# W1 in halves of five DMAs, epsilon folded into the statistics, the last tile in three pieces, 1/den spread by DMA: four edits to a fused attention and MLP kernel

## Chip, cores, metric

The kernel runs on one core of one Trainium2 chip. The metric is the device time of one execution in microseconds (us), lower is better. Each execution also has a span, from the first to the last instruction of the core; for nearly every kernel here the time is about 1.7 us more than the span of the same run.

## The reference

```python
# x: [1, 2048, 640] bf16; wqkv [640, 1920]; wo [640, 640]; w1 [640, 1536]; w2 [1536, 640]; 32 heads of 20
xn = layernorm(x, eps=1e-5)                      # no scale, no bias
q, k, v = split_heads(xn @ wqkv)
phi = lambda t: where(t > 0, t + 1, exp(t)) + 1e-6
kv  = einsum("bhsd,bhse->bhde", phi(k), v)
z   = phi(k).sum(over s)
att = (phi(q) @ kv) / (phi(q) . z + 1e-6)        # "den" is the denominator
out = x + att @ wo + (gelu(xn @ w1 + b1) @ w2 + b2)
```

## The kernel before

Tokens are cut into 16 tiles of 128 rows, and into 4 chunks of 4 tiles. A small recording layer puts each instruction on one of five engines in program order and adds semaphore waits where a resource that it reads or writes has another engine as its last user. A later instruction of an engine never overtakes an earlier one.

Loads. W1 comes in four quarters of its 1536 columns (480 KB each, rows of 768 B), the first on ScalarE's queue, the others between the x tiles on SyncE's:

```python
NW1 = 4
FW = F // NW1
def dma_w1(i, eng="sync"):
    dma_w(eng, W1[:, :, i * FW:(i + 1) * FW], w1v[:, :, i * FW:(i + 1) * FW], r_W1[i])
dma_x(0, 1)
dma_w("scalar", b1tmp[:], ..., r_b1tmp)
dma_w1(0, "scalar")
dma_x(1, 1)
dma_w1(1)
dma_x(2, 1)
dma_w1(2)
dma_x(3, 1)
dma_w1(3)
dma_x(4, 2)
...
```

Layernorm of a tile: two `bn_stats` and a `bn_aggr` on VectorE, then epsilon and the power -1/2 on POOL, then the normalize on VectorE. `ln_next(t)` puts the statistics of tile t+1 ahead of the normalize of tile t:

```python
def ln_aggr(t):
    s = t % 4
    Pl.ins(v, lambda e: e.bn_aggr(aggr[:, s, :], stats[:, s, :]), ...)
    Pl.ins(g, lambda e: e.tensor_single_scalar(veps[:, s:s + 1], aggr[:, s, 1:2], EPS, ALU.add), ...)
    Pl.ins(g, lambda e: e.tensor_tensor(out=rstd[:, s:s + 1], in0=veps[:, s:s + 1],
                                        in1=mhalf[:], op=ALU.pow), ...)
def ln_next(t):
    if t + 1 < NT:
        ln_half(t + 1, 0); ln_half(t + 1, 1)     # bn_stats, waits for x tile t+1
    ln_norm(t)
    if t + 1 < NT:
        ln_aggr(t + 1)
```

The first stage on TensorE (PE): ten warm-up matmuls, then transposes of normalized tiles and "units". A unit is five matmuls that make 128 columns of the hidden layer, followed by a Gelu on ScalarE. A unit waits for the portion of W1 that holds its columns. The first three units are `h_first`; tile 2 is transposed only after units 6 and 7:

```python
filler(10)
ln_stats(0); ln_half(1, 0); ln_half(1, 1); ln_aggr(1)
norm0(...)            # normalize of tile 0 in two parts, after tile 1's statistics
... transposes of tile 0 ...
b1_step()
ln_norm(1)
h_first([0, 1, 2])
xnT_copy(1, transp(1))
ln_stats(2); ln_next(2)                  # statistics(2), statistics(3), normalize(2)
units(0, 1, 3, 2 * JQ)                   # JQ = 3: tile 0, units 3 to 5
units(1, 1, 0, 2 * JQ)                   # tile 1, units 0 to 5
units(0, 2, 2 * JQ, 2 * JQ + 2)          # tiles 0 and 1, units 6 and 7
xnT_copy(2, transp(2))                   # the transposes of tile 2
units(0, 2, 2 * JQ + 2, JT)
```

The last stage adds, per token tile, 12 W2 matmul pairs and 5 attention matmul pairs into two PSUM banks. Before a chunk's attention matmuls its phi(q), held in `PQ`, is multiplied by 1/den, which a matmul with the 0/1 matrix `E4` spreads from 32 partitions to 128:

```python
def rden_step(c, b):
    Pl.ins("tensor", lambda e: e.matmul(bank(b), E4[:, c, :], rden[:], start=True, stop=True), ...)
    Pl.ins("scalar", lambda e: e.activation(rs, bank(b), ACT.Copy), ...)
    for j in range(DT):
        Pl.ins(v, lambda e, j=j: e.tensor_tensor(out=PQ[:, j, cc], in0=PQ[:, j, cc], in1=rs, op=ALU.mult), ...)
def out_last(t):                          # the last tile, in two halves of 320 columns
    for h in range(2):
        ... 17 matmuls, one addition with x, one output DMA ...
for (waits, fns, ev, dma) in list(Pl.records["sync"]):
    if dma and ev is not None:
        Pl.wait_event("sync", ev)         # at the end SyncE waits for every DMA it issued
```

Of the kernel before, what the change touches and what calls it, by code (L numbers as in the profile page):

```python
# [112 lines left out]
def bass_parallel_sum__linear_attn_block__dense_activation_gelu__prompt_kernel(  # L113
# [23 lines left out]
    with contextlib.ExitStack() as es:  # L137
# [34 lines left out]
        veps = sb("veps", [P, 4], FP32)  # L172
# [34 lines left out]
        NW1 = 4  # L207
        r_W1 = [R_("W1_%d" % i) for i in range(NW1)]
# [3 lines left out]
        r_stats = [R_("stats%d" % i) for i in range(4)]  # L212
        r_aggr = [R_("aggr%d" % i) for i in range(4)]
        r_veps = [R_("veps%d" % i) for i in range(4)]
# [26 lines left out]
        def dma_w1(i, eng="sync"):  # L241
            dma_w(eng, W1[:, :, i * FW:(i + 1) * FW], w1v[:, :, i * FW:(i + 1) * FW], r_W1[i])
        dma_x(0, 1)
        dma_w("scalar", b1tmp[:], B_b1.rearrange("(a p) -> a p", p=P), r_b1tmp)
        dma_w1(0, "scalar")
        dma_x(1, 1)
        dma_w1(1)
        dma_x(2, 1)
        dma_w1(2)
        dma_x(3, 1)  # L250
        dma_w1(3)
# [59 lines left out]
        def ln_half(t, h):  # L311
            s = t % 4
            Pl.ins(v, lambda e: e.bn_stats(stats[:, s, 6 * h:6 * h + 6], x_in[:, t, h * HW:(h + 1) * HW]),  # L313
                   reads=[r_x[t]], writes=[r_stats[s]])

        def ln_aggr(t):
            s = t % 4
            Pl.ins(v, lambda e: e.bn_aggr(aggr[:, s, :], stats[:, s, :]),
                   reads=[r_stats[s]], writes=[r_aggr[s]])
            Pl.ins(g, lambda e: e.tensor_single_scalar(veps[:, s:s + 1], aggr[:, s, 1:2], EPS, ALU.add),  # L320
                   reads=[r_aggr[s]], writes=[r_veps[s]])
            Pl.ins(g, lambda e: e.tensor_tensor(out=rstd[:, s:s + 1], in0=veps[:, s:s + 1],
                                                in1=mhalf[:], op=ALU.pow),
                   reads=[r_veps[s], r_small], writes=[r_rstd[s]])
# [27 lines left out]
        def h_unit(t0, n, jb):  # L352
# [6 lines left out]
                reads=[r_W1[jb * P // FW]] + r_xnT[t0:t0 + n], writes=[B_[b]])  # L359
# [22 lines left out]
        def h_first(jbs):  # L382
            bs = [take(1) for _ in jbs]
            for (ks, res) in (((0, 1), r_xnTA), ((2, 3, 4), r_xnT[0])):
                for jb, b in zip(jbs, bs):
                    Pl.ins("tensor", [(lambda e, k=k, jb=jb, b=b: e.matmul(
                        bank(b, 0, P), W1[:, k, jb * P:(jb + 1) * P], xnT[:, k, 0:P],
                        start=(k == 0), stop=(k == DT - 1))) for k in ks],
                        reads=[r_W1[jb * P // FW], res], writes=[B_[b]])
# [20 lines left out]
        b1_step()  # L410
# [23 lines left out]
        units(0, 1, 3, 2 * JQ)  # L434
        units(1, 1, 0, 2 * JQ)
        units(0, 2, 2 * JQ, 2 * JQ + 2)
        xnT_copy(2, transp(2))
        units(0, 2, 2 * JQ + 2, JT)
        ln_next(3)
        ln_next(4)  # L440
        units(2, 1, 0, JQ)
        xnT_copy(3, transp(3))
        units(2, 1, JQ, JT)
# [40 lines left out]
        Pl.ins(v, lambda e: e.memset(KVT, 0.0), writes=[r_KVT] + r_W1)  # L484
        for f in range(DT):
            b = take(2)
            for t in range(NT):
# [5 lines left out]
                   reads=B_[b:b + 2], writes=[r_GT[f]] + r_W1)  # L493
# [71 lines left out]

        def rden_step(c, b):
            cc = slice(c * CW, (c + 1) * CW)
            s = c % 3
            rs = ek[:, s, 0:CW]
            Pl.ins("tensor", lambda e: e.matmul(bank(b), E4[:, c, :], rden[:], start=True, stop=True),  # L570
                   reads=[r_E4, r_rden], writes=[B_[b]])
            Pl.ins("scalar", lambda e: e.activation(rs, bank(b), ACT.Copy), reads=[B_[b]], writes=[r_ek[s]])  # L572
            for j in range(DT):
                Pl.ins(v, lambda e, j=j: e.tensor_tensor(out=PQ[:, j, cc], in0=PQ[:, j, cc], in1=rs, op=ALU.mult),  # L574
                       reads=[r_ek[s], r_PQ[c][j]], writes=[r_PQ[c][j]])

        def x_again(c):
            src = xv[c * CW:(c + 1) * CW, :].rearrange("(t p) d -> p t d", p=P)
            Pl.ins("sync", lambda e: e.dma_start(x_res[:, c * CH:(c + 1) * CH, :], src),
                   writes=[r_xr[c]] + r_xnT, dma=True)  # L580
# [15 lines left out]

        def mm(b, t, i, h):
            tok = slice(t * P, (t + 1) * P)
            l, r = ((HG[:, i, tok], W2[:, i, :]) if i < JT else (PQ[:, i - JT, tok], Msb[:, i - JT, :]))
# [25 lines left out]
        def out_last(t):  # L625
            b = take(2)
            xb(t)
            for h in range(2):
                hs = slice(h * HW, (h + 1) * HW)
                Pl.ins("tensor", [mm(b, t, i, h) for i in range(JT + DT)],  # L630
                       reads=[r for i in range(JT + DT) for r in mm_reads(t, i)], writes=[B_[b + h]])
                Pl.ins(v, lambda e, h=h, hs=hs: e.tensor_tensor(
                    out=out_sb[:, h, 0:HW], in0=bank(b + h, 0, HW), in1=x_res[:, t, hs], op=ALU.add),
                    reads=[B_[b + h], r_xb[t]], writes=[r_out[h]])
                Pl.ins("sync", lambda e, h=h, hs=hs: e.dma_start(ov[t * P:(t + 1) * P, hs], out_sb[:, h, 0:HW]),
                       reads=[r_out[h]], dma=True)
# [5 lines left out]
        out_w2(2, JT // 2, JT, bs[2])  # L642
        for t in range(3):
            out_fin(t, bs[t])
        for t in range(3, NT - 1):
            b = out_w2(t)
            if t in (3, 6, 10):
                rden_step({3: 1, 6: 2, 10: 3}[t], take(1))
            out_fin(t, b)
        out_last(NT - 1)  # L650

        for (waits, fns, ev, dma) in list(Pl.records["sync"]):
            if dma and ev is not None:
                Pl.wait_event("sync", ev)
# [36 lines left out]
```

## Time and profile before

| kernel before | us |
|---|---|
| time, median of the first three runs | 211.89 (211.79 to 212.27) |
| the profiled run: time, span | 212.41, 210.7 |
| PE busy | 205.5 (98%) |
| transposes of tile 2 start | 12.32 |
| last PE instruction ends | 207.80 |

The page of the kernel before, its first and fourth parts: busy time of each engine, and the chain of work that ended last, as shares of the span.

```profile
PE 205.5 (98%) x1585; PEld 140.1 (67%) x1585; DVE 110.5 (52%) x226; ACT 76.8 (36%) x145; POOL 20.5 (10%) x61
PE 86%; DVE 7%; DMA 4%; SPq 1%; issue 1%; DVEq 0%
```

PE is the bound, so a microsecond counts only where PE waits, where PE has fewer instructions, or after PE's end. PE waits at the start. The timeline of the kernel before, first 14 us (start, length, engine, line, operation, out<-in, shapes, count; in brackets the idle time before it and what ended that):

```profile
4.51 0.23 POOL L320 TENSOR_SCALAR veps<-aggr 128x1 f32<-128x1 f32 x1 [2.80 <-DVE aggr L318]
4.82 0.57 POOL L322 TENSOR_TENSOR rstd<-veps,mhalf 128x1 f32<-128x1 f32 x1
5.34 0.21 DVE L318 BATCH_NORM_AGGREGATE aggr<-stats 128x2 f32<-128x12 f32 x1
5.47 0.71 DVE L369 TENSOR_SCALAR xn_tm<-xPK,aggr,rstd 128x256 bf16<-128x256 bf16 x2
5.83 0.29 PE L376 MATMUL ps<-ident,xn_tm 128*128 128x128 bf16 x2
...
6.63 1.22 PE L386 MATMUL ps<-xnT,W 128*128 128x128 bf16 x15
7.68 0.44 PE L340 MATMUL ps<-ident,xn_tm 128*128 128x128 bf16 x5
8.48 3.78 PE L356 MATMUL ps<-xnT,W 128*128 128x128 bf16 x55 [0.35 <-DMA W<-in_B_w_dram]
...
10.88 1.02 DVE L313 BATCH_NORM_STATS2 stats<-xPK 128x6 f32<-128x320 bf16 x2 [0.69 <-DMA xPK<-in_A_x_dram]
11.82 0.43 DVE L333 TENSOR_SCALAR xn_tm<-xPK,aggr,rstd 128x640 bf16<-128x640 bf16 x1
...
12.32 0.45 PE L340 MATMUL ps<-ident,xn_tm 128*128 128x128 bf16 x5
```

Read it backwards from 12.32: the transposes of tile 2 wait for its normalize (11.82), which stands in VectorE's order behind the statistics of tile 3 (10.88), which waited for x tile 3 to land. PE itself was just done with its units. At 8.48 PE had waited 0.35 us for W1's second quarter. The normalize of tile 0 (5.47) starts as soon as tile 1's aggregation (5.34) lets it; its rsqrt (4.82 + 0.57 = 5.39) was only just ready as well.

The end of the chain of waits of the kernel before (start, length, what):

```profile
141.20 0.21 PE ps L570
141.41 8.96 PE ps L600 x66
150.38 0.22 PE ps L570
...
164.45 0.22 PE ps L570
...
183.14 0.22 PE ps L570
183.35 24.46 PE ps L600 x180
...
207.84 0.49 DVE out_sb L632
```

L570 is the spreading matmul. It is on the chain four times, between gapless matmuls. After the last addition the output DMA was issued by 208.69 and landed at 209.94; then SyncE was still going through its waits until 210.23, and the span ended at 210.66.

### The profile page before, as it was taken

Reading aid. Unit: us, or ns where it says so; the run is one execution under the profiler, and the core shown is the slowest. Engines: PE = TensorE matmul, PEld = TensorE weight load, DVE = VectorE, ACT = ScalarE, POOL = GpSimd, SP = SyncE. Lnnn points to the kernel's source line nnn. Section 1 sums busy time; section 2 is a strip of 40 time slices with the busy share of each in tenths; the row PEclk is TensorE's granted clock in tenths of the full one; section 3 lists DMA queues with packets and bytes.
Section 4 is the critical chain, followed back from the end, with each engine's and each line's share of the span. In section 5 each row is a group of like instructions: output and inputs, shape, how many; then the busy total and the mean of one; then the engine's idle time right before and its main releaser. Section 6 shows DMA issues by size and latency. Waiting matters only on the chain.

```text
span 210.7 us, 3883 instructions
## 1 busy us (share of the span) xinstructions
PE 205.5 (98%) x1585; PEld 140.1 (67%) x1585; DVE 110.5 (52%) x226; ACT 76.8 (36%) x145; POOL 20.5 (10%) x61
## 2 busy tenths in 40 slices
PE   7999999999999999999999999999999999999994
PEld 2689987444457777777666555677777777777772
DVE  4689981000008888999078866468451522263221
ACT  2579887666676554111253575110100100100000
POOL 2244557700000000000000000000000000000000
PEclk9999999999999999999999999999999999999999
DMA  5994758999000000000000000355411010001011
GB/s 165 340 349 99 101 111 101 347 321 346 10 0 0 0 3 0 0 3 0 0 0 3 0 5 0 124 138 170 163 35 54 9 65 31 31 31 34 31 62 33
DMA packets 21787, 17.46 MB, mean 83 GB/s; under 512 B 8713, under 2 KB 21769, under 8 KB 21769
## 3 DMA queue, kind: packets, MB, share of 16 engines
q1 hardware_dynamic: 21088, 16.72, 27.6%
q10 hardware_dynamic: 680, 0.49, 0.9%
q8 instruction: 12, 0.20, 0.4%
q14 instruction: 7, 0.05, 0.1%
HBM read 12.62 MB, written 2.62 MB: 72 GB/s over the span
## 4 chain that ended last, share of the span: by engine, by line
PE 86%; DVE 7%; DMA 4%; SPq 1%; issue 1%; DVEq 0%
PE ps L600 35%; PE ps L356 23%; PE ps L477 10%; PE ps L488 10%; PE ps L510 5%; DMA xPK<-in_A_x_dram 4%; DVE PQ L467 3%; DVE ek L465 1%; DVE W L534 1%; SPq L232 1%; PE ps L530 1%; PE ps L546 1%; DVE ZB L524 1%; PE ps L556 1%; DVE stats L313 0%
## 5 line engine op out<-in xcount | busy, mean ns | idle before, releaser
L600 PE MATMUL ps<-W,HG 128*128 128x320 bf16 x384 | 54.9, 299 | 0.0
L356 PE MATMUL ps<-xnT,W 128*128 128x128 bf16 (+2 forms) x435 | 52.0, 282 | 0.4 <-DMA W<-in_B_w_dram 0.4
L600 PEld LDWEIGHTS ps<-W,HG 128*128 128x128 bf16 x384 | 37.5, 98 | 15.2 <-issue 0.4
L356 PEld LDWEIGHTS ps<-xnT,W 128*128 128x128 bf16 x435 | 35.5, 98 | 16.1 <-DMA W<-in_B_w_dram 0.5
L360 ACT ACTIVATE HG<-ps,b1c 128x128 bf16<-128x128 f32 (+2 forms) x87 | 40.0, 492 | 13.2 <-PE ps L356 11.1
L465 DVE TENSOR_SCALAR ek<-ek 128x512 bf16<-128x512 bf16 (+1 forms) x36 | 10.9, 304 | 40.2 <-ACT ek L464 39.1
L464 ACT ACTIVATE ek<-ps 128x512 bf16<-128x512 f32 (+1 forms) x36 | 23.2, 644 | 20.4 <-PE ps L510 11.2
L619 DVE TENSOR_TENSOR out_sb<-ps,xnT 128x640 bf16<-128x640 f32 x15 | 12.4, 825 | 29.3 <-PE ps L600 26.2
L600 PE MATMUL ps<-Msb,PQ 128*128 128x320 bf16 x160 | 24.2, 299 | 0.0
L510 PE MATMUL ps<-xnT,Wqkv 128*128 128x512 bf16 x100 | 22.1, 379 | 0.0
L477 PE MATMUL ps<-Wqkv,xnT 128*128 128x320 bf16 x160 | 21.9, 299 | 0.0
L488 PE MATMUL ps<-xPK,xn_tm 128*128 128x320 bf16 x160 | 21.9, 299 | 0.0
L572 ACT ACTIVATE ek<-ps 128x512 bf16<-128x512 f32 x4 | 2.4, 597 | 49.2 <-PE ps L570 49.2
L600 PEld LDWEIGHTS ps<-Msb,PQ 128*128 128x128 bf16 x160 | 15.6, 98 | 6.3
L477 PEld LDWEIGHTS ps<-Wqkv,xnT 128*128 128x128 bf16 x160 | 15.7, 98 | 6.2
L488 PEld LDWEIGHTS ps<-xPK,xn_tm 128*128 128x128 bf16 x160 | 15.7, 98 | 6.1
L510 PEld LDWEIGHTS ps<-xnT,Wqkv 128*128 128x128 bf16 x100 | 11.6, 118 | 9.5 <-issue 0.2
L313 DVE BATCH_NORM_STATS2 stats<-xPK 128x6 f32<-128x320 bf16 x32 | 15.2, 475 | 3.5 <-DMA xPK<-in_A_x_dram 2.9
L467 DVE SCALAR_TENSOR_TENSOR PQ<-ps,ek 128x512 bf16<-128x512 f32 x20 | 13.8, 692 | 2.1
L467 DVE SCALAR_TENSOR_TENSOR xPK<-ps,ek 128x640 bf16<-128x640 f32 x16 | 13.2, 825 | 1.7
L498 DVE TENSOR_TENSOR Msb<-Msb,xPK 128x640 f32<-128x640 f32 x14 | 11.6, 825 | 0.5
L574 DVE TENSOR_TENSOR PQ<-PQ,ek 128x512 bf16<-128x512 bf16 x20 | 7.1, 419 | 9.0 <-ACT ek L572 9.0
(64 smaller groups left out, 89.3 us busy)
## 6 DMA issues: line engine op xcount, KB each, us to landing
xnT<-in_A_x_dram SPq DMA_DIRECT2D x4, 640.0 KB, 4.1
Wqkv<-in_A_wqkv_dram SPq DMA_DIRECT2D x3, 800.0 KB, 6.9
out_dram<-out_sb SPq DMA_DIRECT2D x15, 160.0 KB, 1.8
W<-in_B_w_dram SPq DMA_DIRECT2D x1, 1920.0 KB, 15.3
W<-in_B_w_dram SPq DMA_DIRECT2D x3, 480.0 KB, 7.6
xPK<-in_A_x_dram SPq DMA_DIRECT2D x2, 640.0 KB, 9.3
Wo<-in_A_wo_dram SPq DMA_DIRECT2D x1, 800.0 KB, 10.5
xPK<-in_A_x_dram SPq DMA_DIRECT2D x4, 160.0 KB, 4.5
```

Source lines behind the costliest of these rows:

```text
L313: Pl.ins(v, lambda e: e.bn_stats(stats[:, s, 6 * h:6 * h + 6], x_in[:, t, h * HW:(h + 1) * HW]), reads=[r_x[t]], writes=[r_stats[s]])
L356: Pl.ins("tensor", [(lambda e, k=k: e.matmul(bank(b, 0, w), W1[:, k, jb * P:(jb + 1) * P], xnT[:, k, tok], start=(k == 0), stop=(k == DT - ...
L360: Pl.ins("scalar", lambda e: e.activation(HG[:, jb, tok], bank(b, 0, w), ACT.Gelu_apprx_tanh, bias=b1c[:, jb:jb + 1]), reads=[B_[b], r_b1c ...
L464: Pl.ins("scalar", lambda e: e.activation(e2, src, ACT.Exp), reads=br, writes=[r_ek[s]])
L465: Pl.ins(v, lambda e: e.tensor_scalar(et, et, 1.0, 1e-6, ALU.min, ALU.add), reads=[r_ek[s]], writes=[r_ek[s]])
L467: Pl.ins(v, lambda e: e.scalar_tensor_tensor(out=d2, in0=src, scalar=0.0, in1=e2, op0=ALU.max, op1=ALU.add), reads=br + [r_ek[s]], writes= ...
L477: fns.append(lambda e, k=k, h=h, b=b, t=t: e.matmul(bank(b + h, 0, HW), xnT[:, k, t * P:(t + 1) * P], Wqkv[:, k, D + h * HW:D + (h + 1) * ...
L488: Pl.ins("tensor", [(lambda e, t=t, h=h, b=b, f=f: e.matmul(bank(b + h, 0, HW), xn_tm[:, t, f * P:(f + 1) * P], PK[:, t, h * HW:(h + 1) * ...
L498: Pl.ins(v, lambda e, t=t: e.tensor_tensor(out=zsum, in0=zsum, in1=PK[:, t, :], op=ALU.add), reads=[r_PK[t], r_zsum], writes=[r_zsum])
L510: Pl.ins("tensor", [(lambda e, k=k, j=j, b=b: e.matmul(bank(b), Wqkv[:, k, j:D:DT], xnT[:, k, cc], start=(k == 0), stop=(k == DT - 1))) fo ...
L600: return lambda e: e.matmul(bank(b + h, 0, HW), l, r[:, h * HW:(h + 1) * HW], start=(i == 0), stop=(i == JT + DT - 1))
L619: Pl.ins(v, lambda e: e.tensor_tensor(out=halves(out_sb[:, s, :]), in0=pair(b), in1=halves(x_res[:, t, :]), op=ALU.add), reads=B_[b:b + 2] ...
```

## The change

Its intent: fewer, longer rows for W1 and single 128-row slices for the first units to wait on; one POOL step less between aggregation and rsqrt; three PE matmuls less; a shorter end. The diff, cut to its core:

```diff
-        NW1 = 4
-        r_W1 = [R_("W1_%d" % i) for i in range(NW1)]
+        NW1 = 2
+        r_W1 = [[R_("W1_%d_%d" % (i, k)) for k in range(DT)] for i in range(NW1)]
...
-        def dma_w1(i, eng="sync"):
-            dma_w(eng, W1[:, :, i * FW:(i + 1) * FW], w1v[:, :, i * FW:(i + 1) * FW], r_W1[i])
+        def dma_w1(i):
+            for k in range(DT):
+                dma_w("sync", W1[:, k, i * FW:(i + 1) * FW], w1v[:, k, i * FW:(i + 1) * FW], r_W1[i][k])
         dma_x(0, 1)
-        dma_w1(0, "scalar")
         dma_x(1, 1)
+        dma_w1(0)
+        dma_x(2, 1)
         dma_w1(1)
-        dma_x(2, 1)
-        dma_w1(2)
         dma_x(3, 1)
-        dma_w1(3)
...
         def ln_half(t, h):            # after bn_stats of the first half
+            if h == 0:
+                Pl.ins(g, lambda e: e.tensor_single_scalar(stats[:, s, 2:3], stats[:, s, 2:3], D * EPS, ALU.add), ...)
         def ln_aggr(t):
-            Pl.ins(g, ... veps = aggr + EPS ...)
             Pl.ins(g, ... rstd = pow(...)) # now of aggr itself
...
         # h_first: waits for the slices W1[i][k] that it reads; b1_step moved behind its matmuls
-        units(0, 2, 2 * JQ, 2 * JQ + 2)    # JQ = 3
+        units(0, 2, JQ, JQ + 2)            # JQ = 6: the same units
...
+        def rden_dma(c):
+            for i in range(4):
+                Pl.ins("sync", lambda e, i=i: e.dma_start(rdb(c)[i:P:4, :], rden[H * c:H * (c + 1), :]), ...)
         def x_again(c):
-                   writes=[r_xr[c]] + r_xnT, dma=True)
+                   writes=[r_xr[c]] + (r_xnT if c == 0 else []), dma=True)
...
         def out_last(t):
-            for h in range(2):             # 320, 320 columns
+            for i, w in enumerate((HW, 3 * 64, P)):   # 320, 192, 128 columns
...
-                rden_step({3: 1, 6: 2, 10: 3}[t], take(1))
+                rden_scale({3: 1, 6: 2, 10: 3}[t])    # only the multiplies
...
-        for (waits, fns, ev, dma) in list(Pl.records["sync"]):
-            if dma and ev is not None:
-                Pl.wait_event("sync", ev)
+        for (waits, fns, ev, dma) in Pl.records["sync"][-3:]:
+            Pl.wait_event("sync", ev)
```

Below, these are called the W1 part, the epsilon part, the 1/den part and the tail part.

More of the change, by code (lines that the diff above doesn't have):

```diff
@@ L171, in bass_parallel_sum__linear_attn_block__dense_activation_gelu__prompt_kernel @@
         aggr = sb("aggr", [P, 4, 2], FP32)
-        veps = sb("veps", [P, 4], FP32)
         rstd = sb("rstd", [P, 4], FP32)
@@ L211, in bass_parallel_sum__linear_attn_block__dense_activation_gelu__prompt_kernel @@
         r_ident, r_small, r_masks, r_bmask, r_E4, r_warm = R_("ident"), R_("small"), R_("masks"), R_("bmask"), R_("E4"), R_("warm")
-        r_stats = [R_("stats%d" % i) for i in range(4)]
+        r_stats = [[R_("stats%d_%d" % (i, h)) for h in range(2)] for i in range(4)]
         r_aggr = [R_("aggr%d" % i) for i in range(4)]
-        r_veps = [R_("veps%d" % i) for i in range(4)]
         r_rstd = [R_("rstd%d" % i) for i in range(4)]
@@ L313, in ln_half @@
             Pl.ins(v, lambda e: e.bn_stats(stats[:, s, 6 * h:6 * h + 6], x_in[:, t, h * HW:(h + 1) * HW]),
-                   reads=[r_x[t]], writes=[r_stats[s]])
+                   reads=[r_x[t]], writes=[r_stats[s][h]])
+            if h == 0:
+                Pl.ins(g, lambda e: e.tensor_single_scalar(stats[:, s, 2:3], stats[:, s, 2:3], D * EPS, ALU.add),
+                       reads=[r_stats[s][0]], writes=[r_stats[s][0]])
         def ln_aggr(t):
@@ L318, in ln_aggr @@
             Pl.ins(v, lambda e: e.bn_aggr(aggr[:, s, :], stats[:, s, :]),
-                   reads=[r_stats[s]], writes=[r_aggr[s]])
-            Pl.ins(g, lambda e: e.tensor_single_scalar(veps[:, s:s + 1], aggr[:, s, 1:2], EPS, ALU.add),
-                   reads=[r_aggr[s]], writes=[r_veps[s]])
-            Pl.ins(g, lambda e: e.tensor_tensor(out=rstd[:, s:s + 1], in0=veps[:, s:s + 1],
+                   reads=r_stats[s], writes=[r_aggr[s]])
+            Pl.ins(g, lambda e: e.tensor_tensor(out=rstd[:, s:s + 1], in0=aggr[:, s, 1:2],
                                                 in1=mhalf[:], op=ALU.pow),
-                   reads=[r_veps[s], r_small], writes=[r_rstd[s]])
+                   reads=[r_aggr[s], r_small], writes=[r_rstd[s]])
         def ln_stats(t):
@@ L358, in h_unit @@
                 start=(k == 0), stop=(k == DT - 1))) for k in range(DT)],
-                reads=[r_W1[jb * P // FW]] + r_xnT[t0:t0 + n], writes=[B_[b]])
+                reads=r_W1[jb * P // FW] + r_xnT[t0:t0 + n], writes=[B_[b]])
             Pl.ins("scalar", lambda e: e.activation(
@@ L388, in h_first @@
                         start=(k == 0), stop=(k == DT - 1))) for k in ks],
-                        reads=[r_W1[jb * P // FW], res], writes=[B_[b]])
+                        reads=[r_W1[jb * P // FW][k] for k in ks] + [res], writes=[B_[b]])
+            b1_step()
             for jb, b in zip(jbs, bs):
@@ L409, in bass_parallel_sum__linear_attn_block__dense_activation_gelu__prompt_kernel @@
         Pl.ins("scalar", lambda e: e.activation(dB, sB, ACT.Copy), reads=[B_[bB]], writes=[r_xnT[0]])
-        b1_step()
         ln_norm(1)
@@ L433, in bass_parallel_sum__linear_attn_block__dense_activation_gelu__prompt_kernel @@
         ln_next(2)
-        units(0, 1, 3, 2 * JQ)
-        units(1, 1, 0, 2 * JQ)
-        units(0, 2, 2 * JQ, 2 * JQ + 2)
+        units(0, 1, 3, JQ)
+        units(1, 1, 0, JQ)
+        units(0, 2, JQ, JQ + 2)
         xnT_copy(2, transp(2))
-        units(0, 2, 2 * JQ + 2, JT)
+        units(0, 2, JQ + 2, JT)
         ln_next(3)
         ln_next(4)
-        units(2, 1, 0, JQ)
+        units(2, 1, 0, 3)
         xnT_copy(3, transp(3))
-        units(2, 1, JQ, JT)
+        units(2, 1, 3, JT)
         units(3, 1, 0, JT)
@@ L481, in bass_parallel_sum__linear_attn_block__dense_activation_gelu__prompt_kernel @@
             phi(pair(b), b, 2, PK[:, t, :], r_PK[t], [r_x[t]])
-        Pl.ins(v, lambda e: e.memset(KVT, 0.0), writes=[r_KVT] + r_W1)
+        Pl.ins(v, lambda e: e.memset(KVT, 0.0), writes=[r_KVT] + [r for q in r_W1 for r in q])
         for f in range(DT):
@@ L492, in bass_parallel_sum__linear_attn_block__dense_activation_gelu__prompt_kernel @@
             Pl.ins("scalar", lambda e, b=b, f=f: e.activation(halves(GTb[:, f, :]), pair(b), ACT.Copy),
-                   reads=B_[b:b + 2], writes=[r_GT[f]] + r_W1)
+                   reads=B_[b:b + 2], writes=[r_GT[f]] + [r for q in r_W1 for r in q])
         Pl.ins(v, lambda e: e.tensor_tensor(out=zsum, in0=PK[:, 0, :], in1=PK[:, 1, :], op=ALU.add),
@@ L564, in den_step, with rden_scale, rdb @@
             return b
+        def rden_scale(c):
+            cc = slice(c * CW, (c + 1) * CW)
+            for j in range(DT):
+                Pl.ins(v, lambda e, j=j: e.tensor_tensor(out=PQ[:, j, cc], in0=PQ[:, j, cc], in1=rdb(c), op=ALU.mult),
+                       reads=r_rdb[c] + [r_PQ[c][j]], writes=[r_PQ[c][j]])
+        ekf = ek[:].rearrange("p a d -> p (a d)")
+        r_rdb = [[R_("rdb%d_%d" % (c, i)) for i in range(4)] for c in range(NC)]
+        def rdb(c):
+            return ekf[:, c % 3 * CW:(c % 3 + 1) * CW]
         def rden_step(c, b):
-            cc = slice(c * CW, (c + 1) * CW)
-            s = c % 3
-            rs = ek[:, s, 0:CW]
             Pl.ins("tensor", lambda e: e.matmul(bank(b), E4[:, c, :], rden[:], start=True, stop=True),
                    reads=[r_E4, r_rden], writes=[B_[b]])
-            Pl.ins("scalar", lambda e: e.activation(rs, bank(b), ACT.Copy), reads=[B_[b]], writes=[r_ek[s]])
-            for j in range(DT):
-                Pl.ins(v, lambda e, j=j: e.tensor_tensor(out=PQ[:, j, cc], in0=PQ[:, j, cc], in1=rs, op=ALU.mult),
-                       reads=[r_ek[s], r_PQ[c][j]], writes=[r_PQ[c][j]])
+            Pl.ins("scalar", lambda e: e.activation(rdb(c), bank(b), ACT.Copy), reads=[B_[b]],
+                   writes=r_rdb[c] + r_ek)
+            rden_scale(c)
+        def rden_dma(c):
+            for i in range(4):
+                Pl.ins("sync", lambda e, i=i: e.dma_start(rdb(c)[i:P:4, :], rden[H * c:H * (c + 1), :]),
+                       reads=[r_rden], writes=[r_rdb[c][i]] + ([r_rdb[0][i]] if c == 3 else []), dma=True)
         def x_again(c):
@@ L594, in bass_parallel_sum__linear_attn_block__dense_activation_gelu__prompt_kernel, with mm_ops @@
             x_again(c)
+        r_out3 = R_("out3")
+        def mm_ops(t, i):
+            tok = slice(t * P, (t + 1) * P)
+            return ((HG[:, i, tok], W2[:, i, :]) if i < JT else (PQ[:, i - JT, tok], Msb[:, i - JT, :]))
         def mm(b, t, i, h):
-            tok = slice(t * P, (t + 1) * P)
-            l, r = ((HG[:, i, tok], W2[:, i, :]) if i < JT else (PQ[:, i - JT, tok], Msb[:, i - JT, :]))
+            l, r = mm_ops(t, i)
             return lambda e: e.matmul(bank(b + h, 0, HW), l, r[:, h * HW:(h + 1) * HW],
@@ L625, in out_last @@
         def out_last(t):
-            b = take(2)
             xb(t)
-            for h in range(2):
-                hs = slice(h * HW, (h + 1) * HW)
-                Pl.ins("tensor", [mm(b, t, i, h) for i in range(JT + DT)],
-                       reads=[r for i in range(JT + DT) for r in mm_reads(t, i)], writes=[B_[b + h]])
-                Pl.ins(v, lambda e, h=h, hs=hs: e.tensor_tensor(
-                    out=out_sb[:, h, 0:HW], in0=bank(b + h, 0, HW), in1=x_res[:, t, hs], op=ALU.add),
-                    reads=[B_[b + h], r_xb[t]], writes=[r_out[h]])
-                Pl.ins("sync", lambda e, h=h, hs=hs: e.dma_start(ov[t * P:(t + 1) * P, hs], out_sb[:, h, 0:HW]),
-                       reads=[r_out[h]], dma=True)
+            lo = 0
+            for i, w in enumerate((HW, 3 * 64, P)):
+                b = take(1)
+                o = out_sb[:, (0, 1, 0)[i], (0, 0, HW)[i]:(0, 0, HW)[i] + w]
+                hs = slice(lo, lo + w)
+                lo += w
+                fns = []
+                for q in range(JT + DT):
+                    l, r = mm_ops(t, q)
+                    fns.append(lambda e, l=l, r=r, q=q, b=b, hs=hs, w=w: e.matmul(
+                        bank(b, 0, w), l, r[:, hs], start=(q == 0), stop=(q == JT + DT - 1)))
+                Pl.ins("tensor", fns, reads=[r for q in range(JT + DT) for r in mm_reads(t, q)], writes=[B_[b]])
+                Pl.ins(v, lambda e, b=b, hs=hs, w=w, o=o: e.tensor_tensor(
+                    out=o, in0=bank(b, 0, w), in1=x_res[:, t, hs], op=ALU.add),
+                    reads=[B_[b], r_xb[t]], writes=[r_out3 if i == 2 else r_out[i]])
+                Pl.ins("sync", lambda e, hs=hs, o=o: e.dma_start(ov[t * P:(t + 1) * P, hs], o),
+                       reads=[r_out3 if i == 2 else r_out[i]], dma=True)
         bs = [out_w2(0)]
@@ L642, in bass_parallel_sum__linear_attn_block__dense_activation_gelu__prompt_kernel @@
         out_w2(2, JT // 2, JT, bs[2])
+        rden_dma(1)
         for t in range(3):
@@ L647, in bass_parallel_sum__linear_attn_block__dense_activation_gelu__prompt_kernel @@
             if t in (3, 6, 10):
-                rden_step({3: 1, 6: 2, 10: 3}[t], take(1))
+                rden_scale({3: 1, 6: 2, 10: 3}[t])
             out_fin(t, b)
+            if t in (3, 7):
+                rden_dma({3: 2, 7: 3}[t])
         out_last(NT - 1)
-        for (waits, fns, ev, dma) in list(Pl.records["sync"]):
-            if dma and ev is not None:
-                Pl.wait_event("sync", ev)
+        for (waits, fns, ev, dma) in Pl.records["sync"][-3:]:
+            Pl.wait_event("sync", ev)
         with contextlib.ExitStack() as ses:
```

## The prediction

> **What bounds the kernel now.** The page's first part has TensorE (PE) busy 205.5 of 210.7 us (98%); the chain of waits puts 86% of the span on it. By the timeline PE runs warm-up matmuls to 5.70 us, starts real work at 5.83, and is then gapless but for 0.35 us at 8.1 to 8.48 (waiting for W1's second quarter) and 0.4 us near 125; it ends at 207.80. The median is 1.2 us above the span.
>
> **Middle: -0.65 us, surest.** Three 128x512 broadcast matmuls (0.21 to 0.22 us each on the chain) go. Their DMAs have time to spare: 1/den is written by 140.3, chunk 1's multiplies started at 151.3, so a copy issued at about 140.5, even behind the x reloads (now issued without waiting for each other), lands long before.
>
> **End: -0.35 us.** The last evacuation, 320 wide, took 0.49 us; 128 wide about 0.3 (the 140-wide one at the KV mask takes 0.31): -0.2. Pieces of 192 and 128 columns cost PE about 17 x (80 + 58) ns against 17 x 136 (128-wide matmuls run 56 to 58 ns apart): +0.1. The last DMA landed at 209.94, but SyncE's string of waits for about 50 DMAs (60 ns a pair, one gap of 0.45) ended only at 210.23: -0.25. The last DMA becomes 256 B packets; the Trainium skill ("DMA: Bandwidth & Descriptors", Specifications) says under 512 B the engine does read-modify-write; no trace here shows it, and with 8 packets per engine I count 0.
>
> **Start: +0.4 us, unsure in sign.**
> - Epsilon: tile 0 loses one POOL step between aggregation and rsqrt (0.31 us with handover). But its normalize at 5.47 also stood behind tile 1's statistics in VectorE's order (busy 4.34 to 5.55): nothing gained, first transposes within 0.1 of 5.83.
> - W1: a quarter (480 KB) sufficed for the first units and landed at 6.30; the next, at 8.43, stopped PE until 8.48. Now 960 KB are needed first, in five steps on one queue; the last lands, I estimate, at 6.9 to 8.1. The first units wait there, the following 45 matmuls don't.
> - Packets: 768 B took 36 ns, 1280 B 55; 1536 B extrapolates to 64, so W1 takes 5.2 instead of 5.8 us of 16 engines, if the memory gives more than the 350 GB/s already reached.
> - x tile 3 is the catch: it stood behind 2080 KB (itself counted) and landed at 10.86; now behind all of W1, 2560 KB, which landed at 12.34; minus up to 0.6 for packets and fewer stalls: 11.5 (10.9 to 12.0). VectorE puts normalize(2) behind statistics(3), so PE's transposes of tile 2, at 12.32 before with 0.06 us of slack, move to x3 + 1.45: about 12.9, after a PE gap of 0.3 to 0.7. The shift then stays.
>
> **Sum:** -0.65 - 0.35 + 0.4 = -0.6: **211.3 us**, 8 in 10 between 210.5 and 212.1. Faster by over 2% 0.01, within 2% 0.98, slower 0.01.
>
> **Shows right or wrong:** landings of x3 and W1 in the DMA issues; PE's gap before tile 2's transposes; first transposes still at 5.8; no PE idle before tiles 4, 8, 12; from PE's end to the span's end 2.86 before, about 2.4 after.
>
> **Would make it wrong:** the early DMA rate (250 to 300 GB/s before 6.5 us) improving or worsening with ten small DMAs; 256 B writes landing slowly; late 1/den copies.

## The result and the profile after

The changed kernel took 211.68 us (median of 4, 211.43 to 212.03) against 211.98 for the kernel before in the same rounds. A ratio is the mean time of one kernel's fast runs over that of the other's of the same rounds, so it is not quite the ratio of the medians: here 0.9986, 95% interval [0.9967, 1.0005]. In a later set with more runs of both it was 0.9997 [0.9982, 1.0011]. It is the same within 2%, and hardly faster at all.

The two profiles, however, have spans of 210.7 and 209.9. The timeline of the changed kernel, first 14 us:

```profile
4.47 0.57 POOL L320 TENSOR_TENSOR rstd<-aggr,mhalf 128x1 f32<-128x1 f32 x1 [0.48 <-DVE aggr L318]
5.27 0.21 DVE L318 BATCH_NORM_AGGREGATE aggr<-stats 128x2 f32<-128x12 f32 x1
5.40 0.71 DVE L367 TENSOR_SCALAR xn_tm<-xPK,aggr,rstd 128x256 bf16<-128x256 bf16 x2
5.75 0.39 PE L374 MATMUL ps<-ident,xn_tm 128*128 128x128 bf16 x2
...
6.61 0.49 PE L384 MATMUL ps<-xnT,W 128*128 128x128 bf16 x6
7.73 0.66 PE L384 MATMUL ps<-xnT,W 128*128 128x128 bf16 x9 [0.63 <-DMA W<-in_B_w_dram]
8.44 0.45 PE L338 MATMUL ps<-ident,xn_tm 128*128 128x128 bf16 x5
8.73 3.77 PE L354 MATMUL ps<-xnT,W 128*128 128x128 bf16 x55
...
11.42 0.89 DVE L310 BATCH_NORM_STATS2 stats<-xPK 128x6 f32<-128x320 bf16 x2 [0.89 <-DMA xPK<-in_A_x_dram]
12.22 0.43 DVE L331 TENSOR_SCALAR xn_tm<-xPK,aggr,rstd 128x640 bf16<-128x640 bf16 x1
12.71 0.45 PE L338 MATMUL ps<-ident,xn_tm 128*128 128x128 bf16 x5 [0.21 <-DVE xn_tm L331]
```

The rsqrt of tile 0 is ready 0.35 us sooner (4.47 + 0.57 = 5.04), and its normalize still waits for tile 1's aggregation, until 5.40. PE waits 0.63 us for the rest of W1's first half and reaches the following units at 8.73 instead of 8.48. Tile 3's statistics start at 11.42 instead of 10.88, and the transposes of tile 2 at 12.71 instead of 12.32: +0.39 us.

The changed kernel's chain of waits from its one spreading matmul to PE's end, and then its last additions and output DMAs in its timeline:

```profile
141.58 0.22 PE ps L577
141.80 61.12 PE ps L616 x450
202.92 4.67 PE ps L652 x51
```

```profile
206.23 2.04 SPq L658 DMA_DIRECT2D out_dram<-out_sb  x3
206.67 0.36 DVE L655 TENSOR_TENSOR out_sb<-ps,xnT 128x192 bf16<-128x192 f32 x1 [0.47 <-PE ps L652]
207.62 0.29 DVE L655 TENSOR_TENSOR out_sb<-ps,xnT 128x128 bf16<-128x128 f32 x1 [0.59 <-PE ps L652]
```

One spreading matmul is left, and from 141.80 on PE never waits. The last addition takes 0.29 us instead of 0.49. The last DMA was issued from 207.94 to 208.27 and landed at 209.39, the waits ended at 209.43, the span at 209.87.

### The profile page after: what moved, and what is told of

Read it like the earlier page. It is cut to its first block, busy times and chain, and to the rows that moved or that the text cites. A ratio compares the mean times of both kernels' runs of the same rounds, so it can differ in the third digit from the quotient of the medians.

```text
span 209.9 us, 3961 instructions
## 1 busy us (share of the span) xinstructions
PE 205.0 (98%) x1599; PEld 140.9 (67%) x1599; DVE 108.7 (52%) x227; ACT 74.9 (36%) x142; POOL 20.2 (10%) x61
## 3 DMA queue, kind: packets, MB, share of 16 engines
HBM read 12.62 MB, written 2.62 MB: 73 GB/s over the span
## 4 chain that ended last, share of the span: by engine, by line
PE 86%; DVE 6%; SPq 3%; DMA 2%; issue 1%; DVEq 0%
PE ps L616 33%; PE ps L354 23%; PE ps L475 10%; PE ps L486 10%; PE ps L508 5%; DVE PQ L465 3%; PE ps L652 2%; DMA xPK<-in_A_x_dram 2%; SPq L234 2%; DVE ek L463 1%; DVE W L532 1%; PE ps L528 1%; PE ps L544 1%; SPq L230 1%; DVE ZB L522 1%
## 5 line engine op out<-in xcount | busy, mean ns | idle before, releaser
L616 PE MATMUL ps<-W,HG 128*128 128x320 bf16 x360 | 51.4, 299 | 0.0
L616 PEld LDWEIGHTS ps<-W,HG 128*128 128x128 bf16 x360 | 35.1, 98 | 14.2 <-issue 0.4
L616 PE MATMUL ps<-Msb,PQ 128*128 128x320 bf16 x150 | 22.5, 299 | 0.0
L616 PEld LDWEIGHTS ps<-Msb,PQ 128*128 128x128 bf16 x150 | 14.6, 98 | 5.7
L310 DVE BATCH_NORM_STATS2 stats<-xPK 128x6 f32<-128x320 bf16 x32 | 13.5, 465 | 2.9 <-DMA xPK<-in_A_x_dram 2.9
L490 ACT ACTIVATE W<-ps 128x640 bf16<-128x640 f32 x5 | 3.5, 704 | 18.2 <-PE ps L486 14.6
L320 POOL TENSOR_TENSOR rstd<-aggr,mhalf 128x1 f32<-128x1 f32 x16 | 9.1, 569 | 8.9 <-DVE aggr L318 8.9
```

The costliest lines, as they stand in the source:

```text
L310: Pl.ins(v, lambda e: e.bn_stats(stats[:, s, 6 * h:6 * h + 6], x_in[:, t, h * HW:(h + 1) * HW]), reads=[r_x[t]], writes=[r_stats[s][h]])
L616: return lambda e: e.matmul(bank(b + h, 0, HW), l, r[:, h * HW:(h + 1) * HW], start=(i == 0), stop=(i == JT + DT - 1))
```

## The experiments

Each experiment is one kernel beside runs of the kernel before on the same chip; four kernels went in each set. Two sums make the traces comparable. The first is the time from the start of tile 2's transposes to the end of the last PE instruction; the second is from there to the end of the span. In microseconds:

| kernel | tile 2's transposes | then to PE's end | then to the span's end | time, median | ratio to before, 95% |
|---|---|---|---|---|---|
| before | 12.32 | 195.49 | 2.85 | 211.98 | |
| before_again | 12.50 | 195.49 | 2.86 | 212.16 | 0.9993 [0.9959, 1.0027] |
| w1_only | 12.75 | 195.50 | 2.62 | 212.89 | 1.0053 [1.0005, 1.0100] |
| den_only | 12.26 | 194.83 | 2.86 | 211.43 | 0.9959 [0.9923, 0.9996] |
| tail_only | 11.87 | 195.53 | 2.52 | 211.91 | 0.9982 [0.9944, 1.0019] |
| eps_only | 12.62 | 195.48 | 2.86 | 211.96 | 0.9994 [0.9980, 1.0009] |
| changed | 12.71 | 194.87 | 2.29 | 211.68 | 0.9986 [0.9967, 1.0005] |
| after_again | 12.57 | 194.89 | 2.29 | 211.90 | 0.9997 [0.9982, 1.0011] |
| x3_early | 13.22 | 194.87 | 2.29 | 212.10 | 0.9995 [0.9983, 1.0007] |
| half_one_dma | 12.52 | 194.86 | 2.29 | 213.38 | 1.0048 [1.0002, 1.0093] |
| old_w1 | 11.67 | 194.87 | 2.30 | 210.89 | 0.9934 [0.9922, 0.9946] |
| quarter_sync | 11.92 | 194.89 | 2.32 | 210.64 | 0.9934 [0.9921, 0.9947] |
| old_w1_x3 | 12.30 | 194.88 | 2.31 | 210.89 | 0.9948 [0.9936, 0.9960] |
| quarter_five | 13.37 | 197.14 | 2.31 | 214.57 | 1.0121 [1.0104, 1.0137] |

The middle column is the finding that makes the rest readable: from tile 2's transposes to PE's end every kernel with the old 1/den takes 195.5 us within 0.03, every one with the new 1/den 194.86 within 0.03 (quarter_five apart, which stalls later as well). In these traces nothing after 13 us varies. What varies from run to run of one kernel lies in the first 13 us, where DMAs land.

The traces also show what varies there. The semaphore of a DMA is updated 16 times, and the DMA counts as landed at the last of them. In the eight traces with W1 in quarters of one DMA, the eighth update of the second quarter came at 6.5 to 7.2 us, but the last one anywhere from 7.70 (old_w1) to 8.89 (eps_only). So it is the last part of a DMA that comes early or late; why is not shown.

One caution for the column of ratios. Six runs took 1.3 to 4.1 us more than the median of the other runs of their kernel, and these six alone have a clock of 0.984 to 0.992: one of the kernel before in the first set (214.30), two of w1_only, three of half_one_dma. A clock of 0.992 over 210 us is worth 1.7 us (an estimate from these readings), so a good part of the excess may go with the clock and not with the edits; none of the six has a trace. Without them the ratios are 1.0034 for w1_only, 0.9972 for den_only, 0.9993 for tail_only and, from three runs, 0.9982 for half_one_dma.

### before_again: the control

No edit.

> The kernel before, unchanged, as a control. The profile of before has a span of 210.7 us in a run of 212.41 us, which is 0.43 above the median 211.98 of its timed runs, so I hold it for a sample from the slow side of the ordinary spread. Theory: span plus a constant 1.7 us is the run's time, the spans of repeated runs spread over about 0.5 us, their median is about 210.25, and the spread comes from the first 13 us (landing of early DMAs). Rival: the profile is typical and about 0.4 us of what the profiles gain is lost outside the span; then the spans here stay at 210.6 to 210.7 with times near 212.0. Ratio to before 1.000 within 0.002 in both.

Measured: the spans of 39 runs of the kernel before, over three chips, lie between 209.9 and 212.5, median 210.4. The profiled run (210.66, time 212.41) is on the slow side, and so is the profile of this control (210.85, time 212.61). In these runs the time stays about 1.7 us above the span, so nothing is lost outside the span. The theory's direction holds; the median is a little higher than I had put it, and the spread wider (1.2 us without the run at 212.5, one of the six at a lower clock). Only one trace is kept per kernel, so for the other runs the start must be inferred: the span less what follows tile 2's transposes (195.49 + 2.85 = 198.34). On the chip of the third set that gives 210.3 - 198.34 = 11.96 for the kernel before, and, from the six runs of the changed kernel there (median span 210.0, and 197.17 after tile 2's transposes), 12.83. By this inference the change costs the start about 0.9 us, not the 0.39 that the pair of profiles shows. Done for every kernel (half_one_dma by its three runs at full clock), it puts the starts of those with quarters of one DMA at 11.59 to 12.30 and of those with halves at 12.55 to 13.24: they do not overlap.

### w1_only, den_only, tail_only, eps_only: one part at a time

w1_only has the two W1 hunks and the moved b1 transpose of the diff above on the kernel before, and nothing else.

> Only the W1 part of the change (two halves of five DMAs, and the b1 transpose moved behind the first units). Theory: slower by about 0.4 us, as x tile 3 and the first half of W1 stand behind more bytes: transposes of tile 2 at about 12.7 us instead of 12.3, PE's end shifted by as much, plus 0.2 us at the end as six more DMAs lengthen the final string of waits by three pairs of 60 ns: +0.6 us in all. Rival (the shift at the start comes from the epsilon sums on POOL): no shift at 12.3, time +0.2.

Measured: 212.89 against 211.98, more than expected. Tile 2's transposes at 12.75, as in the changed kernel, with 0.84 us of PE idle at 7.06 waiting for W1's first half, and 0.09 us before the transposes. The longer string of waits cost nothing here: SyncE was through with it at 210.44, 0.05 after the last landing at 210.39, so the end was 0.24 shorter than before, not 0.2 longer. Two of the six runs took 214.1 and 215.3, at a clock of 0.992; the other four have a median of 212.8. The moved b1 transpose takes 0.11 us of PE's time behind the wait (8.49 to 8.60); it was not tried apart.

den_only has the 1/den part alone; its edit, cut to the last lines (`rden_dma(1)` stands after the W2 matmuls of tile 2):

```diff
...
-                rden_step({3: 1, 6: 2, 10: 3}[t], take(1))
+                rden_scale({3: 1, 6: 2, 10: 3}[t])
             out_fin(t, b)
+            if t in (3, 7):
+                rden_dma({3: 2, 7: 3}[t])
```

> Only the 1/den part (DMAs for chunks 1 to 3, x reloads without waiting for each other). Theory: PE loses three matmuls of 0.21 us, so PE's end comes 0.65 us earlier; but the final string of waits is not shortened in this kernel and gets twelve more DMAs, six pairs of 60 ns, +0.35: about -0.3 us in time. Rival (PE's saved time is taken back by waiting for scaled PQ tiles or for the copies): PE idle before tiles 4, 8 or 12 and PE's end not 0.65 earlier.

Measured: from tile 2's transposes to PE's end 194.83 instead of 195.49, which is the 0.66 us of three matmuls, and PE has no idle time in the last stage. The copies are not late: in the changed kernel those of chunk 1 landed between 143.52 and 145.39 and were first used at 148.36. The time fell by 0.55, not 0.3, because the end stayed as long as before: the longer string of waits ended 0.28 us after the last landing, against 0.29 in the kernel before. The reason is in the next experiment.

tail_only has the new `out_last` and the waits for the last three DMAs.

> Only the last tile in three pieces and waits for the last three DMAs alone. Theory: PE's end +0.05 us, last evacuation 0.29 instead of 0.49, last DMA from issue to landing 1.45 instead of 1.58, end of waits 0.25 sooner: span from PE's end 2.86 to 2.3, time -0.5 us. Rival (the 256 B packets land slower than 640 B ones, or the unread waits cost nothing): time within 0.2 us of before.

Measured: PE's end +0.04, the last addition 0.29 us, the last landing 1.44 us after the start of the issue. But the span still ended 0.72 us after the landing, as before, and the time was 211.91, hardly better than 211.98. Two things hide the gain. The start of these runs was slow: their median span, 210.35, less the constants 195.53 and 2.52, puts tile 2's transposes at 12.3, and the profile's 11.87 is of a run with the shortest of their spans. And SyncE stopped for 0.46 us between its final drain (209.44) and its last instruction (209.90), after all other engines had ended at 209.65; that this falls partly outside what the time counts is suggested by times only 1.43 to 1.50 above the span, instead of 1.7, in five of the six runs (the sixth, 212.95, is 2.65 above its span; why is open). In the kernel before, the same kind of stop lies inside the string of waits (208.99 to 209.44), and without it the string would have been through at about 209.78, before the landing at 209.94. The number of waits counts too, but less: from the last issue to its end the string took 1.54 us in the kernel before with the stop, and without one 1.30 in w1_only (six more DMAs) and 1.53 in den_only (twelve more). An 8 KB instruction packet starts less than 0.7 us from the end of the span in exactly the kernels that stop there (before at 210.06, before_again at 210.27, eps_only at 210.36, tail_only at 210.54). w1_only and den_only have no such packet after 202 us, and their longer strings of waits run without a stop. In the changed kernel the span ends 0.48 after the landing. So trimming the waits is worth 0.24 us, but it depends on where the instruction stream happens to be cut. The packet starts 0.62 to 0.64 us after the stop's end in all four, so the stop does not wait for the arrival of this packet; that the two go together is seen four times out of four, but a cause is not shown.

eps_only has the epsilon part alone.

> Only the epsilon part on the kernel before. Theory: rsqrt of tile 0 is ready 0.3 us sooner but its normalize stays behind tile 1's statistics and aggregation in VectorE's order: first transposes at 5.75 to 5.85, time within 0.15 us of before. Rival (the rsqrt chain bounds the start): first transposes 0.3 earlier, time -0.3.

Measured: first transposes at 5.77 instead of 5.83, time 211.96 against 212.18, ratio 0.9994 with 1 inside the interval. The rival is out: the rsqrt is earlier, and the engine that uses it is not free earlier.

### old_w1: the changed kernel without its W1 part

```diff
-        NW1 = 2
+        NW1 = 4
...
         dma_x(0, 1)
+        dma_w1(0, "scalar")          # quarters of one DMA each, as in the kernel before
         dma_x(1, 1)
-        dma_w1(0)
-        dma_x(2, 1)
         dma_w1(1)
+        dma_x(2, 1)
+        dma_w1(2)
         dma_x(3, 1)
+        dma_w1(3)
```

> The changed kernel with its W1 part undone (four quarters, one DMA each, the first on ScalarE's queue; b1 transpose where it was). The control and the parts say that the profile of before had an unlucky start: spans of before lie at 210.0 to 211.1, median 210.25, against 210.66 profiled. So the W1 part costs more than the 0.4 us that the two profiles show. Theory: W1 part +0.9 us, the rest -1.2 us; this kernel is 1.2 us faster than before (210.8 us), 0.9 faster than the changed kernel; tile 2's transposes at 11.8 to 12.5. Rival: W1 costs 0.4 and the parts do not add up (tail and 1/den overlap); then -0.7 us, 211.3.

Measured: 210.89 against 212.18 for before on the same chip, ratio 0.9934. The rest of the change is worth 1.3 us, and the W1 part takes 1.0 to 1.1 of it back, as the whole change gains only 0.16 to 0.30 (ratios 0.9986 and 0.9997 with the W1 part, 0.9934 without). The timeline of PE in old_w1:

```profile
6.94 1.01 PE L385 MATMUL ps<-xnT,W 128*128 128x128 bf16 x15 [0.33 <-DMA W<-in_B_w_dram]
7.79 0.44 PE L339 MATMUL ps<-ident,xn_tm 128*128 128x128 bf16 x5
8.06 3.77 PE L355 MATMUL ps<-xnT,W 128*128 128x128 bf16 x55
11.67 0.44 PE L339 MATMUL ps<-ident,xn_tm 128*128 128x128 bf16 x5
```

### x3_early: x tile 3 ahead of W1's second half

```diff
         dma_x(2, 1)
+        dma_x(3, 1)
         dma_w1(1)
-        dma_x(3, 1)
```

> The changed kernel with x tile 3 sent ahead of W1's second half instead of behind it. Theory in the prediction: x3's place behind all of W1 is what costs. Then x3 lands near 8.7, W1's second half near 11.4, tile 2's transposes no later than PE's own order allows: gain of the gap seen there, 0.2 us in the profile of the changed kernel, 0.5 at most. Rival: the wait for the first half of W1 (0.63 us of PE idle at 7.1) carries the shift; then PE stops for W1's second half instead and nothing is gained.

Measured: x3 landed at 8.23 instead of 11.39, and the kernel got no faster: 212.10 against 212.18. It is the rival's outcome: nothing gained, and PE stops for W1's second half. PE in its timeline:

```profile
7.60 0.66 PE L384 MATMUL ps<-xnT,W 128*128 128x128 bf16 x9 [0.63 <-DMA W<-in_B_w_dram]
...
8.60 2.68 PE L354 MATMUL ps<-xnT,W 128*128 128x128 bf16 x45
12.14 1.25 PE L354 MATMUL ps<-xnT,W 128*128 128x256 bf16 x10 [0.87 <-DMA W<-in_B_w_dram]
13.22 0.44 PE L338 MATMUL ps<-ident,xn_tm 128*128 128x128 bf16 x5
```

Now unit 6 waits 0.87 us for W1's second half, complete at 11.89. Tile 2's transposes come after units 6 and 7 and after x3's statistics; with halves both need x0 to x3 and all of W1, 2560 KB, in whatever order they come. With quarters they need 2080 KB. x3 was the last of those bytes, not the cause.

### half_one_dma, quarter_five, quarter_sync: number of DMAs, and the queue

half_one_dma keeps the halves and sends each in one DMA:

```diff
-            for k in range(DT):
-                dma_w("sync", W1[:, k, i * FW:(i + 1) * FW], w1v[:, k, i * FW:(i + 1) * FW], r_W1[i][k])
+            Pl.ins("sync", lambda e: e.dma_start(W1[:, :, i * FW:(i + 1) * FW], w1v[:, :, i * FW:(i + 1) * FW]),
+                   writes=r_W1[i], dma=True)
```

> The changed kernel with each half of W1 in one DMA of 960 KB instead of five (same bytes, same row length of 1536 B, same order). Theory (bytes ahead set the landings, five DMAs only let the first two slices be used early): x3 lands at the same 11.4 within 0.3, the first units wait until about 7.5 for everything, tile 2's transposes within 0.3 of the changed kernel, time within 0.4. Rival (ten small DMAs and their issues of 0.43 us each slow the queue): x3 lands 0.5 us or more earlier and the time falls by as much.

Measured: in the trace x3 at 11.08, the first half at 7.52, tile 2's transposes at 12.52: within the theory's bounds but for x3, 0.31 earlier than in the changed kernel instead of at most 0.3, and none 0.5 earlier. PE in its timeline:

```profile
7.57 1.01 PE L383 MATMUL ps<-xnT,W 128*128 128x128 bf16 x15 [1.07 <-DMA W<-in_B_w_dram]
...
8.91 3.77 PE L353 MATMUL ps<-xnT,W 128*128 128x128 bf16 x55
12.52 0.44 PE L337 MATMUL ps<-ident,xn_tm 128*128 128x128 bf16 x5
```

Here all of PE's waiting is for the first half; before tile 2's transposes it does not wait. The times were not within the bounds: three of the six runs took 214.2 to 215.6 us, at a clock of 0.992, 0.984 and 0.992. The other three took 211.4 to 212.5, so its median says nothing of the question. The traces kept are of ordinary runs; whether W1 in halves has to do with the long runs (two of six in w1_only, three of six here, none in five of x3_early and in ten of the changed kernel, one in 39 of the kernel before) is left open.

quarter_five has quarters, and each in five DMAs of 96 KB:

```diff
-        NW1 = 2
+        NW1 = 4
         dma_x(1, 1)
         dma_w1(0)
-        dma_x(2, 1)
         dma_w1(1)
+        dma_x(2, 1)
+        dma_w1(2)
         dma_x(3, 1)
+        dma_w1(3)
```

> The changed kernel with W1 in four quarters, each in five DMAs on SyncE's queue (20 DMAs of 96 KB, rows of 768 B), first units waiting for single slices as in the changed kernel. Theory (size of the portion that a unit waits for): x tile 3 is issued at about 11.2 us at the earliest, as the 20 W1 DMAs before and around it take 0.47 us each on SyncE; now issue binds: x3 is the 19th DMA, issued at about 9.3, landing near 11.3, so tile 2's transposes stay near 12.7 and the time is near that of the changed kernel; the second quarter is complete at about 8.0. Rival (many small DMAs are harmless): x3 at 10.2 and time equal to old_w1.

Measured: 214.57, slower by 2.5 us than before: a miss in size, and the rival is wrong too. The queue of SyncE in its timeline, and the rates of its DMAs in windows of 2 us (last column GB/s, the one before it the busy share of the 16 DMA engines):

```profile
1.72 4.69 SPq L234 DMA_DIRECT2D W<-in_B_w_dram  x10
6.45 0.43 SPq L230 DMA_DIRECT2D xPK<-in_A_x_dram  x1
6.93 2.33 SPq L234 DMA_DIRECT2D W<-in_B_w_dram  x5
```

```profile
4.00:6.00 2.00, 2.00 (x7) 0.47 (x5) 1.73 (x7) 0.00 (x0) 1.28 (x3) 1.00 0.78 212
6.00:8.00 2.00, 1.82 (x24) 1.33 (x24) 0.64 (x3) 0.58 (x2) 0.07 (x1) 1.00 0.84 222
8.00:10.00 2.00, 1.41 (x26) 1.27 (x24) 1.33 (x3) 1.65 (x7) 0.22 (x1) 1.00 0.82 244
```

SyncE issues one DMA every 0.47 us. 96 KB in 0.47 us is 209 GB/s, and the rate from 4 us on is 212 to 244, against about 350 in the other kernels. The Trainium skill ("DMA: Bandwidth & Descriptors", Issuing engines are not separate DMA queues) calls the issue time usually small relative to the DMA; here it is more than the transfer (96 KB at 350 GB/s, an estimate from the traces' rate, is 0.28 us). I had counted the late x3 but not that everything behind it, x tiles 4 and 5 too (16.58), comes late. For the slices of the changed kernel, 192 KB in 0.47 us is 418 GB/s, more than the memory gives, so its issues do not bind.

quarter_sync has whole quarters, all on SyncE's queue; against old_w1:

```diff
-        dma_w1(0, "scalar")
         dma_x(1, 1)
+        dma_w1(0)
```

> The changed kernel with W1 in four quarters of one DMA each, all on SyncE's queue (the same as old_w1 but for the first quarter's queue and its place behind x tile 1). Theory: what the W1 part costs is that a unit must wait for half of W1, and unit 6 for all of it, 2400 KB in place of 1920; the queue does not matter. Then this kernel is within 0.25 us of old_w1 (1.3 us faster than before), W1's second quarter at 7.6 to 8.4, x3 near 10.2, tile 2's transposes at 11.6 to 12.1. Rival: the gain of old_w1 is that the first quarter goes over ScalarE's queue beside x; then it is 0.5 us or more slower than old_w1.

Measured: 210.64, ratio 0.9934, the same as old_w1. The queue does not matter, as the same section of that page says of queues in general (they end on the same 16 engines). PE in its timeline has no wait for W1 at all:

```profile
6.82 1.22 PE L385 MATMUL ps<-xnT,W 128*128 128x128 bf16 x15
...
8.24 3.78 PE L355 MATMUL ps<-xnT,W 128*128 128x128 bf16 x55
11.92 0.45 PE L339 MATMUL ps<-ident,xn_tm 128*128 128x128 bf16 x5
```

### old_w1_x3 and after_again

old_w1_x3 sends x tile 3 ahead of W1's third quarter in old_w1:

```diff
         dma_x(2, 1)
-        dma_w1(2)
         dma_x(3, 1)
+        dma_w1(2)
```

> A candidate to beat both: old_w1 with x tile 3 sent ahead of W1's third quarter. Theory: in old_w1 PE is without a gap from 8.06 on, so neither x3 (10.12) nor the third quarter (9.66) holds it; with x3 at about 8.7 and the third quarter at about 10.1 nothing changes on PE: within 0.2 us of old_w1. Rival (x3 still holds PE in the runs with a slow start): up to 0.3 us faster.

Measured: 210.89, ratio 0.9948: no gain over old_w1, as the theory had it. (Its trace has tile 2's transposes later, at 12.30, because W1's second quarter landed at 8.64 instead of 7.70, and PE waited for that.) after_again is the changed kernel as the control of the third set:

> The changed kernel, unchanged, as a control beside the others: ratio to before 0.9986 measured earlier in four runs. Theory: -0.3 us again, 0.9 slower than old_w1 of the other call; tile 2's transposes at 12.5 to 13.0. Kernels with W1 in halves had single runs of 214 to 215 us (two of six in w1_only, three of six in half_one_dma); whether this one has them too is open, one in six would not surprise me.

Measured: 211.90 against 212.06, and tile 2's transposes at 12.57. The gain was half of that expected, and none of the six runs was an outlier. The versions that beat both kernels are old_w1 and quarter_sync, by 1.3 to 1.4 us against the kernel before.

## Why the prediction was right or wrong

The range held and so did "same within 2%". The centre, 211.3, was 0.4 too low, and the change in time was -0.3 and -0.16 in two sets instead of -0.6. The terms of the sum, in us:

| term | predicted | measured |
|---|---|---|
| three matmuls | -0.65 | -0.66 (den_only) |
| last tile's matmuls | +0.1 | +0.04 (tail_only) |
| last addition | -0.2 | -0.20 |
| last DMA, issue to landing | 0 | -0.13 (1.58 to 1.45) |
| string of waits | -0.25 | -0.24 (span's end: 0.72 to 0.48 after the landing) |
| start | +0.4 | +0.39 between the two profiles; about +0.9 between typical runs |

- **Middle: right.** The matmuls' time came off PE whole, and the copies had time to spare.
- **End: right in sign, a little better than the sum.** "Waiting for 50 DMAs" was costed right from the trace, but for a partly wrong reason: most of it was one stop of 0.45 us, which two other kernels with even more waits don't have. For 256 B packets 0 was close: they took 18 ns, the 640 B ones 32.
- **Epsilon: right.** The first transposes moved by 0.08 us; eps_only shows no gain.
- **Packets: right in the duration, not in the way it helps.** 1536 B packets took 65 ns in the median (64 predicted). But bytes moved by 12 us were 3093 KB after and 3106 before: from 8 to 12 us the rate was 351 to 358 GB/s before, 360 to 376 after, and 352 to 353 in after_again. The Trainium skill ("DMA: Bandwidth & Descriptors", Specifications) gives about 358 GB/s of memory bandwidth for one core, and the two traces of this pair agree within 5% there (single windows of others reach 389, half_one_dma from 6 to 8 us). The prediction made the saving depend on the memory giving more, and no clear rise is seen. The landing did come sooner all the same, by more than the 0.6 allowed: the same 2560 KB were in at 11.39 instead of 12.35, and in all traces at 11.08 to 11.89 with halves against 11.60 to 12.80 with quarters of one DMA. With as many bytes moved, what came sooner is the last of the 16 updates: 1.1 to 1.4 us after the first for the slices of the changed kernel, 2.1 to 2.3 for the quarters on SyncE's queue before. That the row length does this is not shown; but with longer rows the same bytes were not in later, so the row length is not what costs the start.
- **Start: the step that failed is the size, "+0.4 us".** Where tile 2's transposes would be was read well: 12.9 predicted, 12.71 and 12.57 in the two traces, 12.8 inferred for typical runs. Where they were before was taken from one profile, 12.32, and that run was a slow one: typical runs have about 12.0 (inferred from their spans). The sign of it was there to see: the profiled run took 212.41 us, 0.5 more than the median, and "the median is 1.2 us above the span" compared a median with the span of another run. The shift was mis-sized by half, about 0.5 us; the end gave back 0.2 (-0.53 instead of -0.35), and so the sum was off by only 0.3 to 0.4. That the total came this near to the centre owes something to this cancelling, which is luck.
- **"x tile 3 is the catch": half right.** It is what tile 2's transposes wait for in the changed kernel, as predicted, with x3 at 11.39 (11.5 predicted); but PE's gap there was 0.21 us, not 0.3 to 0.7, and moving x3 forward gave nothing (x3_early). The cause is the size of the portion: with halves PE needs 2560 KB before those transposes, with quarters 2080, and old_w1 gets the loss back. The portion acts at a second place, which the prediction saw but did not size: most of PE's waiting in the changed kernel's trace (0.63 of 0.84 us), and all of it in half_one_dma (1.07), is for the rest of the first half, before x3 matters. Its units alone would have ended at 12.50 (8.73 + 3.77), 0.21 before the transposes. No run sizes the two places apart.

Left open: what gave six runs a lower clock and 1.3 to 4.1 us more time, and whether W1 in halves has to do with it; what makes SyncE stop for 0.45 us; why the last part of a DMA comes so late in some runs; and whether another order of PE's units would make halves harmless, which no run tried.

## What to carry to other kernels

When the start of a kernel is bound by loads, count the bytes that must have landed before the first instruction that cannot be put off; a larger portion raises that count, and moving one tensor within the same portions only changes which wait is seen. A DMA must carry more bytes than the memory delivers during its own issue (here 0.47 us), or the issuing engine becomes the bound. And check that the profiled run is a typical one, by its own time against the median, before taking a difference of a few tenths from it: here the stretch that varies is exactly the one that the change touches.

## What the Trainium skill lacked or had wrong

- "DMA: Bandwidth & Descriptors", Specifications: it names 512 B as the smallest transfer for line rate, with read-modify-write below that. In the last output tile 256, 384 and 640 B packets took 18, 22 and 32 ns in the median: a smooth loss per byte (14, 17 and 20 GB/s per engine) and no step at 512 B in these three sizes, and the smallest DMA landed soonest (1.45, 1.50 and 1.58 us after the start of its issue).
- The same page, Issuing engines are not separate DMA queues: "usually small relative to the DMA itself" is not so for DMAs of 96 KB. I found no figure in units of time for an issue on SyncE (a count of cycles for earlier generations stands in its part on trn3 B0); the runs show one each 0.47 us, which held the 16 engines at 212 to 244 GB/s in quarter_five.
- "Runtime: NRT & Kernel Launch", Instruction fetch mechanics: it says that instructions come in 16 KiB blocks and that the cost of crossing one is mostly hidden. The traces have instruction packets of 16 KB and of 8 KB, and SyncE has a stop of about 0.45 us near the end of exactly those four profiles that have an 8 KB packet starting within 0.7 us of the span's end; whether the fetch causes it is not shown.
- No page that I looked at says how much the landing of the first DMAs varies from run to run: one kernel's spans lay between 209.9 and 211.1 (one of 39 at 212.5, at a clock of 0.992), while in the traces PE's time after the start of tile 2's transposes repeated within 0.03 us. Within one DMA the last of 16 semaphore updates came 1.4 to 2.7 us after the first for the second quarter of W1.
